# The last product of an attention and two-MLP kernel as seven block products over pairs of 384-token sets

## The chip, the cores and the metric

The kernel runs on one core of a Trainium2 chip. The metric is the time of one execution on the device, in microseconds (us). Before the change it is 973.07 us, the median of three runs (972.98 to 973.09).

## The reference

Causal block attention (4 batches, 8 heads, 576 positions, head size 64, blocks of 64) gives 2304 tokens of 512 values. Two small networks follow, both in float32:

```python
    a = x @ w1
    b = x @ w2
    h = a * b @ w3
    return (h @ w_out).astype(np.float32)
...
    h = x @ w_in
    alpha = 1.0
    g = np.where(h > 0.0, h, alpha * (np.exp(np.minimum(h, 0.0)) - 1.0))
    return (g @ w_out).astype(np.float32)
```

In the second network x is 2304 x 512, w_in 512 x 2048 and w_out 2048 x 512. The change touches only this second network, above all its last product `g @ w_out`.

## The kernel before, in words

Every float32 matrix product is made of three TensorE passes: each operand is split into a rounded high part (type fp32r) and the low remainder, and the passes are high x high, high x low and low x high (`PASSES`). The high part is written by ACT (a cast, L769), the remainder by POOL (a subtraction, L772).

The work has three stages that overlap at their borders. Stage 1 is the attention. Stage 2 (`block2`, eight sets of 288 tokens) is the first network; its matmuls are the groups a, b (L846) and y (L810), 288 columns wide. Stage 3 (`block3`, from L904) is the second network, in six sets of 384 tokens. In each set there are 16 hidden blocks of 128. For each block, 12 matmuls of 384 columns make `h` (L918: 4 blocks of the inner size times 3 passes, the weights are the stationary operand). DVE takes min(h, 0) (L930), ACT the exponential (L934), DVE joins both to g in place (L939), ACT and POOL split g. Then 9 matmuls of 512 columns (L953: 3 groups of 128 tokens times 3 passes) add this block to three output banks; g is the stationary operand there, and `w_out` the moving one. After block 15 the three banks are copied out (L439 on ACT, L440 on DVE) and written by DMA (L970). That is 1152 `h` matmuls and 864 `o` matmuls in stage 3.

The weights of stage 3 come as float64 words. During stage 2 a chain of small operations turns them into float32 and splits them (`convert`: loads L386, DVE L360 to L368, POOL L374, ACT L405, and the remainder L383 on POOL or DVE). Four of the sixteen weight slabs stay in SBUF (`slab_hi`); twelve go to DRAM (L1034) and come back (L1039) into the slabs of stage 2 as these fall free, once, before or early in stage 3. The inputs of stage 3 are split twice buffered: `xa` for even sets, `xb` for odd ones (L892, L897).

The order of the work is written by a planner (`Plan.run`): it goes through all operations with estimated durations, takes at each moment the ready operation with the lowest `prio` on each engine, and emits each engine's instructions in that order. The engines then run their queues strictly in it. Operations marked `port=True` are laid out so that DVE and POOL never do two of them at once. Some have `ways`, and the planner picks the engine. `TURNS` replaces the priority of single operations by hand-set numbers.

## Time and profile before

| | before |
|---|---|
| time, median of 3 runs | 973.07 us |
| span of the profiled execution (first to last instruction) | 970.1 us |
| PE busy | 960.6 us (99%) |
| DVE, ACT, POOL busy | 511.3, 427.6, 399.2 us |
| PE's granted clock | full speed in every slice of the page |
| stage 3 on PE, from its first stretch of `h` alone to the last `o` | 563.59 to 966.04 us |

The time around the span is 973.07 - 970.1 = 2.97 us. Stage 2 ends at about 563 us: from 557 us on, its last `y` matmuls and the first `h` matmuls alternate.

### The profile page before, as it was taken

What the parts mean: (1) busy time and instruction counts of PE and PEld (TensorE: products, weight loads), DVE (VectorE), ACT (ScalarE), POOL (GpSimd) and SP (SyncE); (2) the same over time, 40 slices, a digit from 0 to 9 for tenths busy, and PEclk for the clock granted to TensorE, in tenths of its full rate; (3) what the DMA queues carried; (4) which work ended last, traced back from release to release, by engine and by line L of the source; (5) the groups of instructions that cost most, each with busy time, mean ns of one, the idle gap of its engine ahead of it and who ended that gap; (6) DMA issues with size and microseconds to landing.
All of it is one profiled execution on the core that took longest, in us unless ns stands there. A gap on an engine that the chain in (4) does not pass through costs nothing.

```text
span 970.1 us, 15899 instructions
## 1 busy us (share of the span) xinstructions
PE 960.6 (99%) x5910; PEld 821.4 (85%) x5910; DVE 511.3 (53%) x1087; ACT 427.6 (44%) x1008; POOL 399.2 (41%) x419
## 2 busy tenths in 40 slices
PE   9999999999999999999999999999999999999998
PEld 4555478788888889999999999998999889888997
DVE  7888988766565556676766342322322322322322
ACT  5867577556656654464454422222222222222222
POOL 6354758323232226666656542332322422422222
PEclk9999999999999999999999999999999999999999
DMA  8554433131122003245465950000000000000000
GB/s 290 195 184 161 160 128 96 54 96 50 50 78 71 27 16 112 95 154 183 171 210 202 391 233 1 1 32 1 23 12 1 25 10 1 33 1 1 33 1 33
DMA packets 41789, 87.61 MB, mean 90 GB/s; under 512 B 6000, under 2 KB 15472, under 8 KB 40176
## 3 DMA queue, kind: packets, MB, share of 16 engines
q1 hardware_dynamic: 41712, 86.60, 25.8%
q8 instruction: 46, 0.75, 0.3%
q14 instruction: 31, 0.25, 0.1%
HBM read 69.21 MB, written 17.38 MB: 89 GB/s over the span
## 4 chain that ended last, share of the span: by engine, by line
PE 93%; DVE 4%; DMA 1%; issue 1%; SPq 1%; POOL 0%; ACT 0%; POOLq 0%; DVEq 0%; ACTq 0%
PE h L918 21%; PE o L953 21%; PE b L846 10%; PE a L846 10%; PE y L810 10%; PE o L675 5%; PE s L549 4%; PE t L585 4%; PE wps L745 4%; PE spare L1054 3%; PE s L611 1%; DVE ct L368 1%; DVE ct L360 1%; PE t L645 1%; DMA scr<-rs 0%
## 5 line engine op out<-in xcount | busy, mean ns | idle before, releaser
L772 POOL TENSOR_TENSOR g<-e,g 128x384 fp32r<-128x384 f32 x96 | 97.4, 1016 | 276.6 <-ACT g L769 262.8
L930 DVE TENSOR_SCALAR e<-h 128x384 f32<-128x384 f32 x96 | 53.4, 557 | 221.6 <-PE h L918 210.1
L953 PE MATMUL o<-slab_lo,g 128*128 128x512 f32 x648 | 162.9, 396 | 0.0
L934 ACT ACTIVATE e<-e 128x384 f32<-128x384 f32 x96 | 50.4, 525 | 232.2 <-DVE e L930 232.2
L953 PEld LDWEIGHTS o<-slab_lo,g 128*128 128x128 f32 x648 | 121.1, 188 | 23.5
L810 PE MATMUL y<-g,slab_lo 128*128 128x288 f32 x768 | 118.9, 300 | 0.5 <-DVE xy L830 0.3
L846 PE MATMUL a<-xs,slab_lo 128*128 128x288 f32 x768 | 117.9, 298 | 0.0
L846 PE MATMUL b<-xs,slab_lo 128*128 128x288 f32 x768 | 117.1, 297 | 0.4 <-DVE af L863 0.4
L810 PEld LDWEIGHTS y<-g,slab_lo 128*128 128x128 f32 x768 | 106.5, 188 | 2.7 <-issue 1.0
L846 PEld LDWEIGHTS b<-xs,slab_lo 128*128 128x128 f32 x768 | 106.7, 188 | 1.4 <-DVE af L863 0.6
L846 PEld LDWEIGHTS a<-xs,slab_lo 128*128 128x128 f32 x768 | 106.9, 188 | 1.0 <-issue 0.3
L772 POOL TENSOR_TENSOR g<-af,g 128x288 fp32r<-128x288 f32 x64 | 56.0, 875 | 80.0 <-ACT g L769 78.4
L918 PE MATMUL h<-xb,slab_lo 128*128 128x384 f32 x432 | 82.1, 339 | 0.0
L918 PE MATMUL h<-xa,slab_lo 128*128 128x384 f32 x432 | 81.5, 336 | 0.0
L939 DVE SCALAR_TENSOR_TENSOR e<-e,h 128x384 f32<-128x384 f32 x96 | 53.1, 554 | 51.2 <-ACT e L934 50.9
L918 PEld LDWEIGHTS h<-xb,slab_lo 128*128 128x128 f32 x432 | 77.1, 188 | 3.0
L918 PEld LDWEIGHTS h<-xa,slab_lo 128*128 128x128 f32 x432 | 76.3, 188 | 3.2 <-DVE e L939 0.2
L769 ACT CAST g<-e 128x384 fp32r<-128x384 f32 x96 | 49.0, 513 | 66.2 <-DVE e L939 58.2
L374 POOL TENSOR_TENSOR ct<-ct,cr 128x512 int32<-128x512 int32 x48 | 65.2, 1362 | 30.3 <-DVE ct L368 11.5
L575 ACT ACTIVATE p<-s,st 128x128 f32<-128x128 f32 (+3 forms) x128 | 67.2, 528 | 16.1 <-DVE st L570 11.4
L570 DVE TENSOR_REDUCE st<-s 128x1 f32<-128x128 f32 (+3 forms) x128 | 61.4, 489 | 5.5 <-PE s L555 2.1
L439 ACT COPY pt<-t 128x512 f32<-128x512 f32 (+4 forms) x91 | 36.8, 409 | 55.9 <-PE t L585 49.1
(89 smaller groups left out, 1455.7 us busy)
## 6 DMA issues: line engine op xcount, KB each, us to landing
cr<-w SPq DMA_DIRECT2D x48, 512.0 KB
wsc<-stage SPq DMA_DIRECT2D x24, 512.0 KB
slab_lo<-wsc SPq DMA_DIRECT2D x12, 1024.0 KB
cr<-w3T SPq DMA_DIRECT2D x16, 512.0 KB
raw<-qT SPq DMA_DIRECT2D x16, 288.0 KB
raw<-kT SPq DMA_DIRECT2D x16, 288.0 KB
out<-ob SPq DMA_DIRECT2D x17, 256.0 KB
cr<-wo SPq DMA_DIRECT2D x8, 512.0 KB
```

Of the source, the lines that this page charges most:

```text
L374: nc.gpsimd.tensor_tensor(out=t(), in0=t(), in1=words()[0], op=ALU.add)
L570: nc.vector.tensor_reduce(out=nm(c), in_=s()[:, 0:nk], axis=AX.X, op=ALU.max, negate=True)
L575: lambda s=s, c=c, p=p: nc.scalar.activation(out=p()[:, 0:nk], in_=s()[:, 0:nk], func=AF.Exp, bias=nm(c), scale=1.0, accum_out=sm(c)),
L769: add("ACT", act_us(n, True), lambda: nc.scalar.copy(g()[:, 0, :], src()), r=[key], w=[(g, 0)], prio=prio)
L772: lambda: nc.gpsimd.tensor_tensor(out=g()[:, 1, :], in0=src(), in1=g()[:, 0, :].bitcast(F32), op=ALU.subtract),
L810: nc.tensor.matmul(ps()[:, 0:T2], lhsT=w[:, a, n * P:(n + 1) * P], rhs=gs[m]()[:, c, :], start=(m == ms[0] and q == 0), stop=(m == ms[-1] ...
L846: nc.tensor.matmul(ps()[:, 0:T2], lhsT=w[:, a, u, k, :], rhs=xs()[:, k, c, :], start=(k == 0 and q == 0), stop=(k == KD - 1 and q == 2),)
L918: nc.tensor.matmul(ph()[:, 0:T3], lhsT=w[:, a, k, :], rhs=xs()[:, k, c, :], start=(k == 0 and q == 0), stop=(k == KD - 1 and q == 2),)
L930: "DVE", dve_us(T3), lambda e=e, ph=ph: nc.vector.tensor_scalar_min(e(), ph()[:, 0:T3], 0.0),
L934: "ACT", act_us(T3, True), lambda e=e: nc.scalar.activation(out=e(), in_=e(), func=AF.Exp),
L939: lambda e=e, ph=ph: nc.vector.scalar_tensor_tensor(out=e(), in0=e(), scalar=-1.0, in1=ph()[:, 0:T3], op0=ALU.add, op1=ALU.max),
L953: nc.tensor.matmul(acc(), lhsT=g()[:, a, s * P:(s + 1) * P], rhs=w[:, c, :], start=(m == 0 and q == 0), stop=(m == KG - 1 and q == 2),)
```

## The change

Two sets of 384 tokens are now worked as a pair, and `g` of a pair and `w_out` are cut into 2 x 2 blocks: the hidden size into halves of 1024, the output into halves of 256, the tokens into the two sets. The product of two such 2 x 2 block matrices needs eight block products; Strassen's identity (in Winograd's form) makes it with seven, p1 to p7, and sums of blocks before and after.

Stage 3 becomes six parts j: three pairs, and for each the hidden size in two steps of four blocks out of each half (`KP = 4`). `part_h(j)` makes 16 hidden blocks (4 q, 2 sets s, 2 halves f) exactly as before up to g, which is now kept unsplit in SBUF (`ga` for even j, `gb` for odd j). `part_o(j)` runs the seven terms of `TERMS`; for each of them and each q a block of g or a sum of blocks (`tt`, on DVE or POOL) is split into `sp` (ACT cast, remainder on POOL or DVE; six buffers), and 2 x 3 matmuls of 384 columns follow. Here the weights are stationary, g moves, and the output comes out transposed (the host turns it back). `post` adds the seven results up with DVE (and a few on POOL). `h` matmuls have four banks in place of two.

The seven weight combinations of `w_out` are made during stage 2 (`w_out_unit`: three subtractions, two ACT casts and four remainder subtractions for each of eight units) and written to DRAM (`wso`, eight units x 2 x 896 KB), as is `w_in` (`wsi`). In stage 3 both are read back piece by piece: 24 loads of `win` and 42 of `wout`, 1 MB each, into three buffers each. The split inputs have one buffer for each set of the pair. The hand-set priorities from operation 2498 on fall away, those before it stay.

```diff
+KP = 4
+NH = 256
+TERMS = ((0, "p1"), (6, "p6"), (2, "p2"), (5, "p7"), (4, "p5"), (1, "p4"), (3, "p3"))
...
-    2368: 17069.46, 2369: 17098.29, 2377: 17057.62, 2414: 17086.71, 2420: 17154.84, 2498: 1324.98, 2520: 2001.81,
...
-    3780: 106909.16, 3792: 106919.16,
+    2368: 17069.46, 2369: 17098.29, 2377: 17057.62, 2414: 17086.71, 2420: 17154.84,
...
-    hi_ring = Ring(late1, "slab_hi", 4, [P, 2, 1024], F32R, "gate1")
-    hi_buf = [hi_ring.next() for _ in range(4)]
...
-    wsc = [dram.tile([P, 2, 1024], F32, name=f"wsc{m}") for m in range(4, KG)]
+    wt_r = Ring(late1, "wt", 2, [P, 7, NH], F32, "gate1")
+    wh_r = Ring(late1, "wh", 2, [P, 7, NH], F32R, "gate1")
+    wsi = [dram.tile([P, 2, 2, HS], F32, name=f"wsi{m}") for m in range(KH)]
+    wso = [dram.tile([7, P, KP, 2, NH], F32, name=f"wso{p}") for p in range(NP)]
...
-    xs3_r = [Ring(late1, "xa", 1, [P, KD, 2, T3], F32R, "gate1"), Ring(late2, "xb", 1, [P, KD, 2, T3], F32R, "gate2")]
-    g3_r = Ring(late2, "g", 4, [P, 2, T3], F32R, "gate2")
...
+    win_r = slabs((8, 9, 10), "win", [P, 2, 2, HS], F32R)
+    wout_r = slabs((11, 6, 7), "wout", [P, KP, 2, NH], F32R)
+    xa_r = Ring(late1, "xa", 1, [P, KD, 2, T3], F32R, "gate1")
+    e_r = Ring(late1, "e", 3, [P, T3], F32, "gate1")
+    xb_r = slabs((4, 5), "xb", [P, 2, 2, T3], F32R)
...
+        ga = slabs((0, 1, 2, 3), "ga", [P, KP + 1, T3], F32)
+        late["ga"] = [ga.next() for _ in range(4)]
+        late["gb"] = Ring(late2, "gb", 1, [P, 4 * KP, T3], F32, "gate2").next()
+        late["sp"] = [after(r, "sp", [P, 2, T3], F32R) for r in (cr2_ring, stage_r, wh_r)]
+        late["ob"] = after(t2_ring, "ob", [P, T3], F32)
+        late["ot"] = [x.next() for x in [after(wt_r, "ot", [P, 4, T3], F32)] for _ in range(2)]
+        late["cp"] = xy_buf(0, "cp", (P, 6, T3))
...
+    def part_h(j, xs):
...
+            for s in range(2):
+                for f in range(2):
+                    ph = turn("h", (4, 5, 6, 7), "h")
...
+                            "PE", 6 * T3 * COL + 0.02, mm, r=[(wb, 0), *xkeys(k0), *xkeys(k0 + 1)], w=[ph],
+                            prio=1e5 + 1000 * j + 240 * q + 120 * s + 60 * f, lag=0.3, big=True,
...
+                        "DVE", dve_us(T3), lambda e=e, ph=ph: nc.vector.tensor_scalar_min(e(), ph()[:, 0:T3], 0.0),
...
+    def part_o(j):
...
+        zb = [bank((0, 2)[n], "oz") for n in range(2)]
+        xb = [bank((1, 3)[n], "ox") for n in range(2)]
...
+        for x, (slot, name) in enumerate(TERMS):
+            wb = wout_r.next()
+            add(
+                "SP", 0, lambda wb=wb, slot=slot: nc.sync.dma_start(out=wb().bitcast(F32), in_=wso[p][slot]),
...
+                if name == "p1":
+                    pr = need + 60
+                    tt(a21, a21, a11, ALU.subtract, [k11], [k21], pr, False)
+                    tt(a21, a21, a22, ALU.add, [k22], [k21], pr, False)
+                if name in ("p7", "p5", "p3"):
+                    s_, ks = sum_next()
+                    u, v, op, ku, kv = {
+                        "p7": (a22, a21, ALU.subtract, k22, k21),
+                        "p5": (a21, a11, ALU.add, k21, k11),
+                        "p3": (a12, a21, ALU.subtract, k12, k21),
+                    }[name]
+                    tt(s_, u, v, op, [ku, kv], [ks], need, False)
+                else:
+                    s_, ks = {"p1": (a11, k11), "p6": (a21, k21), "p2": (a12, k12), "p4": (a22, k22)}[name]
+                sp = split_next()
...
+                    "ACT", act_us(T3, True), lambda sp=sp, s_=s_: nc.scalar.copy(sp()[:, 0, :], s_()), r=[ks],
...
+                    "POOL", 0.17 + T3 * 0.00215,
+                    lambda lo=lo, hi=hi, s_=s_: nc.gpsimd.tensor_tensor(out=lo(), in0=s_(), in1=hi(), op=ALU.subtract),
+                    r=[ks, (sp, 0)], w=[(sp, 1)], prio=need, port=True,
+                    ways=[(
+                        "DVE", dve_us(T3),
...
+                for n in range(2):
+
+                    def mm(n=n, q=q, sp=sp, wb=wb, to=to, first=first, last=last):
+                        w = wb()[:, q]
                             nc.tensor.matmul(
+                                to[n]()[:, 0:T3], lhsT=w[:, a, n * P:(n + 1) * P], rhs=sp()[:, c, :],
...
+                        "PE", 3 * T3 * COL + 0.01, mm, r=[(wb, 0), (sp, 0), (sp, 1)], w=[to[n]],
+                        prio=1e5 + 1000 * (j + 1) + 34 * (KP * x + q) + 17 * n, lag=0.3, big=True,
+                    )
+            for n in range(2):
+                post(j, name, n, V(to[n]), to[n], fast)
-                    w = slab3(m)[:, :, 512:1024]
-                            acc(), lhsT=g()[:, a, s * P:(s + 1) * P], rhs=w[:, c, :],
...
+    def post(j, name, n, acc, ak, fast):
...
+            tt(ob, acc, a, ALU.add, [ak, ka], [ob], fast, True)
+            r0, t0 = (n + 2 * (i % 2)) * P, (A, Bt)[i // 2]
...
+        if name == "p1":
+            evac(T3, p1, acc, [ak], [k1], fast, "ACT")
+        elif name == "p6":
+            tt(u2, acc, p1, ALU.add, [ak, k1], [k2], fast, True)
+            more(u2, k2, 1)
+        elif name == "p2":
+            result(0, None, None)
+        elif name == "p7":
+            tt(u3, acc, p1, ALU.add, [ak, k1], [k3], fast, True)
+            more(u3, k3, 3)
+            more(p1, k1, 2)
+        elif name == "p5":
+            result(3, u3, k3)
+        elif name == "p4":
+            result(2, p1, k1)
+        else:
+            result(1, u2, k2)
...
-    first3 = [block3_in(t) for t in range(2)]
...
+    def w_in_unit(m, prio):
...
+    def w_out_unit(m, prio):
+        wt, wh = wt_r.next(), wh_r.next()
...
+        dtt(lambda t: t[:, 4:6], lambda t: t[:, 1:4:2], lambda t: t[:, 0:2], (0, 1, 3), (4, 5), 512)
+        dtt(lambda t: t[:, 6], lambda t: t[:, 3], lambda t: t[:, 4], (3, 4), (6,), 256)
+        dtt(lambda t: t[:, 1], lambda t: t[:, 2], lambda t: t[:, 6], (2, 6), (1,), 256)
+        for c0, c1 in ((4, 7), (0, 4)):
+            cs = range(c0, c1)
...
+                    "POOL", 0.17 + NH * (x1 - x0) * 0.00215, lambda sub=sub: sub(nc.gpsimd), r=[(wh, x) for x in xs_],
...
+                    out=wso[p_][:, :, q_, c, :].rearrange("i p c -> p i c"), in_=b().bitcast(F32)
...
+    for p in range(NP):
+        for q in range(KP):
+            for f in range(2):
+                w_in_unit(KP * p + q + f * KH, 2000.0 + 20 * p + q)
+        for q in range(KP):
+            w_out_unit(KP * p + q, 2010.0 + 20 * p + q)
+    stage3()
+    for j in range(NP * N3):
+        if j and j % NP == 0:
+            xs3 = [block3_in(j // NP * 2 + s) for s in range(2)]
+        part_h(j, xs3)
+        if j:
+            part_o(j - 1)
+    part_o(NP * N3 - 1)
```

Three places show how the instructions move. The first is PE in the middle of stage 3. Before, for one hidden block: `h` matmuls of one weight slab, then nine `o` matmuls with g as the stationary operand (the number behind `<-` first is the stationary slab or the moving tile, with its buffer number).

```order
L918 MATMUL h_7696<-xb_7037,slab_lo_1340 128x384 x6
L953 MATMUL o_7555<-slab_lo_1254,g_7684 128x512 x3
L953 MATMUL o_7560<-slab_lo_1254,g_7684 128x512 x3
L953 MATMUL o_7566<-slab_lo_1254,g_7684 128x512 x3
L918 MATMUL h_7696<-xb_7037,slab_lo_1340 128x384 x6
L918 MATMUL h_7725<-xb_7037,slab_lo_1417 128x384 x6
```

In the changed kernel, in part 1 of `part_h` and part 0 of `part_o` (`oz`, `ox`, `oy` are the output banks, two of each):

```order
L1069 MATMUL oz_7408<-sp_7500,wout_6860 128x384 x3
L984 MATMUL h_7614<-xb_6968,win_7304 128x384 x6
L984 MATMUL h_7614<-xb_6929,win_7304 128x384 x6
L1069 MATMUL oz_7402<-sp_7528,wout_6860 128x384 x3
L1069 MATMUL oz_7408<-sp_7528,wout_6860 128x384 x3
L1069 MATMUL ox_7486<-sp_7538,wout_7474 128x384 x3
L984 MATMUL h_7650<-xb_6968,win_7304 128x384 x6
L984 MATMUL h_7650<-xb_6929,win_7304 128x384 x6
L1069 MATMUL ox_7492<-sp_7538,wout_7474 128x384 x3
L1069 MATMUL ox_7486<-sp_7566,wout_7474 128x384 x3
```

Groups of three `o` matmuls now stand between groups of twelve `h` matmuls; all are 384 columns wide, and each six of `o` need one `sp`.

The second place is DVE in the middle of stage 3. Before, it only alternates the two operations of a hidden block:

```order
L930 TENSOR_SCALAR e_8558<-h_8507 128x384
L939 SCALAR_TENSOR_TENSOR e_8558<-e_8558,h_8507 128x384
L930 TENSOR_SCALAR e_8594<-h_8568 128x384
L939 SCALAR_TENSOR_TENSOR e_8594<-e_8594,h_8568 128x384
L930 TENSOR_SCALAR e_8623<-h_8587 128x384
```

In the changed kernel, in the last fifth of stage 3, from one `e<-h` on:

```order
L996 TENSOR_SCALAR e_10034<-h_10012 128x384
L1005 SCALAR_TENSOR_TENSOR gb_7434<-e_10034,h_10012 128x384
L1060 TENSOR_TENSOR sp_10057<-ga_7058,sp_10057 128x384
L959 TENSOR_TENSOR ga_7344<-ga_7344 128x384
L959 TENSOR_TENSOR ga_7058<-ga_7058 128x384
L996 TENSOR_SCALAR e_10074<-h_10049 128x384
L432 COPY cp_7641<-oz_9852 128x384
L1005 SCALAR_TENSOR_TENSOR gb_7434<-e_10074,h_10049 128x384
L959 TENSOR_TENSOR gb_7434<-gb_7434 128x384
L959 TENSOR_TENSOR ga_7166<-ga_7166 128x384
```

Remainders (L1060), sums of g blocks (L959) and the joining of results stand between the two operations of a hidden block, in one queue. The remainder into sp_10057 stands behind `h_10012`; PE uses that `sp` four hidden blocks later.

The third place is DVE where stage 2 ends. Before, the last of the weight conversion (`ct`, L368) is done ahead of the first `e`:

```order
L363 TENSOR_SCALAR ct_6823<-ct_6823 128x512
L863 TENSOR_TENSOR af_6833<-b_6825,af_6833 128x288
L368 SCALAR_TENSOR_TENSOR ct_6823<-cr_6746,ct_6823 128x512
L863 TENSOR_TENSOR af_6894<-b_6887,af_6894 128x288
L830 TENSOR_TENSOR xy_3750<-y_6904,xy_3750 128x288
```

In the changed kernel the last weight units (`ct`, `wt`) stand among the first hidden blocks:

```order
L1005 SCALAR_TENSOR_TENSOR ga_7058<-e_7032,h_6983 128x384
L1199 TENSOR_TENSOR wt_6916<-wt_6916 128x512
L1199 TENSOR_TENSOR wt_6916<-wt_6916 128x256
L822 TENSOR_TENSOR xy_3748<-y_7060,xy_3748 128x288
L996 TENSOR_SCALAR e_7088<-h_7048 128x384
L1199 TENSOR_TENSOR wt_6916<-wt_6916 128x256
L1005 SCALAR_TENSOR_TENSOR ga_7058<-e_7088,h_7048 128x384
L996 TENSOR_SCALAR e_7112<-h_7081 128x384
L360 SCALAR_TENSOR_TENSOR ct_7011<-cr_6931,ct_7011 128x512
L1215 TENSOR_TENSOR wt_6916<-wt_6916,wh_7079 128x512
```

The last operation on `wt` in this queue stands behind the thirteenth `e<-h` of stage 3, and the first `o` matmul stands behind 17 of the 96 groups of twelve `h` matmuls on PE.

## Rows read from the trace of the kernel before

**Rows 1.** The page: span, busy time of each engine, PE's clock by slice.
```profile
span 970.1 us, 15899 instructions
PE 960.6 (99%) x5910; PEld 821.4 (85%) x5910; DVE 511.3 (53%) x1087; ACT 427.6 (44%) x1008; POOL 399.2 (41%) x419
...
PEclk9999999999999999999999999999999999999999
```
**Rows 2.** PE's longest waits: releaser, us in total, times, longest us.
```profile
PE spare L1054 <- POOL mk L982: 2.0, 1, 2.0
PE t L585 <- ACT p L575: 1.8, 1, 1.8
PE o L675 <- DVE pt L440: 0.5, 1, 0.5
PE b L846 <- DVE af L863: 0.4, 1, 0.4
...
```
**Rows 3.** Busy us (instructions) by stretch: PE, PEld, DVE, ACT, POOL; clock, DMA share, GB/s.
```profile
300.00:400.00 100.00, 99.72 (x770) 88.79 (x769) 57.60 (x149) 52.10 (x140) 38.83 (x41) 1.00 0.19 62
400.00:500.00 100.00, 99.66 (x747) 99.39 (x746) 72.48 (x121) 49.88 (x103) 64.49 (x60) 1.00 0.49 169
500.00:560.00 60.00, 59.86 (x448) 59.62 (x447) 30.45 (x58) 25.98 (x54) 34.14 (x32) 1.00 0.75 282
562.00:570.00 8.00, 8.00 (x47) 7.45 (x47) 7.37 (x16) 2.13 (x5) 4.05 (x6) 1.00 1.01 422
600.00:700.00 100.00, 100.00 (x500) 90.15 (x499) 31.60 (x58) 26.49 (x51) 32.26 (x32) 1.00 0.03 11
```
**Rows 4.** PE in order of time: start, us, operation, count (an end is modelled).
```profile
535.04 1.76 PE L846 MATMUL a<-xs,slab_lo 128*128 128x288 f32 x12
536.64 1.76 PE L846 MATMUL b<-xs,slab_lo 128*128 128x288 f32 x12
...
563.59 4.33 PE L918 MATMUL h<-xa,slab_hi 128*128 128x384 f32 x24
567.76 2.27 PE L953 MATMUL o<-slab_hi,g 128*128 128x512 f32 x9
...
587.80 2.26 PE L953 MATMUL o<-slab_lo,g 128*128 128x512 f32 x9
589.90 2.26 PE L918 MATMUL h<-xa,slab_lo 128*128 128x384 f32 x12
```
**Rows 5.** The end, in order of time.
```profile
956.03 10.01 PE L953 MATMUL o<-slab_lo,g 128*128 128x512 f32 x42
...
966.13 0.42 DVE L440 COPY ob<-o 128x256 f32<-128x256 f32 x1 [2.17 <-PE o L953]
966.59 0.37 ACT L439 COPY ob<-o 128x256 f32<-128x256 f32 x1 [3.44 <-DVE ob L440]
```
**Rows 6.** Groups from 560 to 970 us: busy us, mean ns; idle before.
```profile
L772 POOL TENSOR_TENSOR g<-e,g 128x384 fp32r<-128x384 f32 x96 | 97.4, 1016 | 276.6 <-ACT g L769 262.8 <-issue 13.8
...
L930 DVE TENSOR_SCALAR e<-h 128x384 f32<-128x384 f32 x96 | 53.4, 557 | 221.6 <-PE h L918 210.1 <-POOL g L772 11.6
L939 DVE SCALAR_TENSOR_TENSOR e<-e,h 128x384 f32<-128x384 f32 x96 | 53.1, 554 | 51.2 <-ACT e L934 50.9
L934 ACT ACTIVATE e<-e 128x384 f32<-128x384 f32 x96 | 50.4, 525 | 232.2 <-DVE e L930 232.2
L769 ACT CAST g<-e 128x384 fp32r<-128x384 f32 x96 | 49.0, 513 | 66.2 <-DVE e L939 58.2 <-PE o L953 8.0
...
L918 PEld LDWEIGHTS h<-xb,slab_hi 128*128 128x128 f32 x144 | 25.7, 188 | 1.1
```
**Rows 7.** Groups from 400 to 575 us, the weight conversion's.
```profile
L374 POOL TENSOR_TENSOR ct<-ct,cr 128x512 int32<-128x512 int32 x26 | 35.2, 1357 | 19.1 <-issue 10.8 <-DVE ct L368 4.3 <-POOL g L772 2.0
...
L383 POOL TENSOR_TENSOR stage<-ct,stage 128x512 fp32r<-128x512 f32 x14 | 19.2, 1371 | 5.0 <-ACT stage L405 5.0
...
L383 DVE TENSOR_TENSOR stage<-ct,stage 128x512 fp32r<-128x512 f32 x10 | 8.9, 890 | 1.6 <-ACT stage L405 1.6
...
L383 DVE TENSOR_TENSOR slab_hi<-ct,slab_hi 128x512 fp32r<-128x512 f32 x2 | 2.0, 1010 | 0.0
```
**Rows 8.** Waits of the queue that issues the DMAs: us, times, longest.
```profile
SPq L386 <- POOL ct L374: 117.3, 36, 7.0
```

## What was predicted

> **What bounds the kernel now.** I read the page first: PE is busy 960.6 of 970.1 us, with its clock at full speed in all 40 slices, while DVE has 53%, ACT 44% and POOL 41% [rows 1]. Since a busy PE need not be PE at its pace, the waits come next: the longest single one is 2.0 us, and none of the listed ones stands in stage 3 [rows 2]. The stretches then show who else could bound a stage: in stage 3 (600 to 700 us) PE is busy for all 100 us, DVE for 31.60, ACT 26.49, POOL 32.26, and the DMAs move 11 GB/s; in stage 2 (400 to 500) DVE has 72.48 and POOL 64.49 [rows 3]. So stage 3 is bound by PE's stream alone, and a matmul column taken out there is time taken out, until another engine's queue is late.
>
> What a column costs follows from the starts of PE's stretches, since the ends are modelled. From 563.59 us [rows 4] to 956.03 + 10.01 = 966.04 [rows 5] PE issues 864 `o` matmuls of 512 columns and 1152 - 12 = 1140 `h` matmuls of 384 (twelve stand before 563.59): 864 x 512 + 1140 x 384 = 880,128 columns in 402.45 us, 0.4573 ns a column. So 384 columns take 175.6 ns, 512 take 234.1 ns. Three stretches confirm that the price goes by columns: 24 `h` take 567.76 - 563.59 = 4.17 us (173.8 ns each), nine `o` take 589.90 - 587.80 = 2.10 us (233 ns), and twelve matmuls of 288 columns in stage 2 take 536.64 - 535.04 = 1.60 us (133 ns) [rows 4].
>
> **The change part by part.** *PE in stage 3.* The 864 `o` matmuls of 512 columns go: 864 x 0.2341 = 202.3 us. In come 3 pairs x 2 steps x 7 terms x 4 blocks x 2 output halves x 3 passes = 1008 of 384 columns: 1008 x 0.1756 = 177.0 us. The 1152 `h` matmuls stay. Sum: -25.3 us. At the 173.8 ns of the pure stretch the whole stage (2160 matmuls) would take 375.4 us against 402.45 + 12 x 0.1756 = 404.6, that is -29.2 us; this is the far end of the gain.
>
> *DVE, POOL and ACT in stage 3.* DVE keeps 96 minima and 96 joinings: 96 x 0.557 + 96 x 0.554 = 106.7 us [rows 6]. The order gives it 85 remainders and 107 sums with two SBUF inputs, 66 additions from PSUM and 3 copies. For a 384-wide addition with a PSUM input the nearest row is the 0.554 us joining [rows 6]. An operation with two SBUF inputs of 384 does not occur: below, 0.554 us; above, the 512-wide remainder at 0.890, or 1.010 for two of them [rows 7]. I take 0.56, since width and type match that row, and keep 1.01 for the range. DVE: 106.7 + 192 x 0.56 + 69 x 0.554 = 252 us of the stage's 379 (67%); at 1.01 it is 339 us (89%). POOL has 83 remainders and 31 sums at 1.016 [rows 6]: 116 us (31%). ACT: 96 x 0.525 + 168 x 0.513 [rows 6] and 15 copies of about the same size: 144 us (38%). None reaches PE's 379 us. In the steady part the six `sp` let a remainder stand four hidden blocks ahead of its use (the order's second place), over 8 us, and four banks hold `h`: a late DVE operation of one microsecond does not reach PE. At the two changes of pair, `xa` is split only after its last use; between that and the first new `h` the order puts 54 matmuls (9.5 us) on PE, and the splits take four or eight POOL operations, some 4 to 5 us by the 1.016 of rows 6. I count 1 us for all of this, 0 to 8.
>
> *The end.* After the last `h` PE has 177 `o` matmuls (31.1 us) and nothing beside them, where before it had 42 (10.01 us [rows 5]). There DVE has about 28 two-input operations and 12 PSUM additions, POOL 12: laid end to end without overlap, 28 x 0.56 + 12 x 0.554 + 12 x 1.016 = 34.5 us; DVE alone 22. A cast, a remainder and a sum per `sp` must keep up with 1.05 us of PE. I count 1 us, 0 to 6. After PE's last matmul come two additions of 0.55 us in place of copies of 0.42 and 0.37 [rows 5], and the same kind of DMA: nothing.
>
> *Weight preparation in stage 2.* Added on DVE: 8 subtractions of 512 and 16 of 256, remainders 20 of 512 and 5 of 256; gone: 7 remainders. At 0.89 for 512 and half for 256: 28 x 0.89 + 21 x 0.45 - 7 x 0.89 = 28 us more, in a stretch (400 to 560) where DVE is busy 72.48 of 100 and 30.45 of 60 us [rows 3]: room for 57. POOL: 9 remainders at 1.371 go and 7 come, about even. The chain is paced by POOL already: the loads wait 117.3 us for it [rows 8]. So preparation runs on into stage 3 (the third place), covered by 17 groups of twelve `h` (17 x 12 x 0.1756 = 35.8 us) that need no `sp`. Behind a DVE operation on `wt` that waits for a DMA stand the minima of the next `h`, and behind these PE once four banks are full (4 x 2.1 us). I count 1 us, 0 to 15.
>
> *DMA.* 66 loads of 1 MB over 379 us are 183 GB/s by count, where the trace reached 422 GB/s at the border of the stages [rows 3]. Each has its buffer free while two others are in use (9 us or more): hidden. Without the cover a load costs about 1.05 MB / 422 GB/s = 2.5 us and its latency.
>
> *Sum*, against the profiled execution: 970.1 - 25.3 + 1 + 1 + 1 = 947.8 us of span, and with the 2.97 us around it, 950.8. **I predict 951 us**, 22 below the median of 973.07.
>
> **The rivals.** *The queue at the border (D).* DVE stands on a weight unit whose DMA is late, and PE runs dry in its first 40 us of stage 3. For it: DVE's and POOL's load in rows 3, the waits of rows 8, the full DMA at 562 us. Against: 35.8 us of cover and priority for the old stage's work. Price 8 to 15 us: 959 to 966 us.
>
> *The end or the collisions (C).* Two-input operations at 0.89 to 1.01: DVE reaches 316 to 339 us of 379 on the mean, and in the last 31 us 28 x 0.89 + 12 x 0.554 = 31.6, so that it paces PE there. For it: in the conversion the 512-wide remainder takes DVE 0.890 and 1.010 us [rows 7], more than its width explains (0.554 x 512 / 384 = 0.74). Against: the planner keeps these operations of DVE and POOL apart. Price 5 to 10 us: 956 to 961. The Trainium skill's page "SBUF — State Buffer", section "SBUF: two separate sides", says that a DVE operation with two SBUF inputs and a GpSimd operation exclude each other for their whole length; the rows of 0.890 and 1.010 agree with it. By that rule the last 31 us hold one queue of 28 x 0.56 + 12 x 1.016 = 27.9 us beside PE's 31.1, and C would come out as the forecast does.
>
> *The weight loads bind (W).* 2160 loads of the stationary operand stand in for 2016. In 600 to 700 us PEld is busy 90.15 us for 499 loads, 180.7 ns each [rows 3]; priced so, stage 3 takes 390.3 us, a gain of only 14.3: 961.8 us with the 3 us. Against: 24 matmuls with 24 loads in 4.17 us, and 769 loads in 88.79 us [rows 3, 4], 115 ns each. The Trainium skill, page "Trainium Kernel Development and Optimization", section "Best Practices", calls the busy share of the weight loads, not that of the matmuls, the measure of how near PE is to its limit. By that rule the stage is 90% full and the price is W's; the trace does not agree, since 288-column matmuls pass at 133 ns.
>
> *DVE becomes the bound (S), slower than before.* In-order DVE takes the stage over if a two-input operation costs more than (404.6 - 106.7 - 38.2) / 192 = 1.35 us on the mean. At 1.5 us the stage lasts 433 us and the kernel 1001. For it: operations lengthen where POOL is busy (1.010). Against: nothing in the rows reaches 1.35.
>
> *The change does not do what it says* is out for PE: the order has the 1008 matmuls of 384.
>
> **How the numbers follow.** Forecast 0.70 (946 to 956 us; with every stall at zero 947.8, or 943.9 at 173.8 ns). C 0.12, D 0.10, W 0.03, S 0.05. The range 945 to 962 us holds the forecast, C, W and the cheap part of D; outside are the pure gain, the dear part of D and S, in all under 0.2. A measurement of this kernel can tell about 0.2% (2 us) from no change. Slower is S, 0.05; 0.02 of D is left for stalls that eat just what is gained, the same; faster is the rest, 0.93.
>
> **What would show it.** Right: 1008 matmuls at 175 ns, PE full from the first `h` to the end, stage 3 some 380 us long; DVE about two thirds busy, two-input operations near 0.56; PE's waits in stage 3 3 us in all. Wrong: PE waiting for DVE or POOL on `sp` in many places (C, S), a gap within 40 us of the first `h` (D), or PE full with `o` at 181 ns (W). A stage 2 longer than before would be outside all of these.

## The result, and the profile after

The changed kernel takes 944.27 us (median of four runs, 942.28 to 946.19); the kernel before, on the same chip, 973.03. The ratio is 0.9717, 95% interval 0.9694 to 0.974. The forecast was 951 us, 945 to 962: the direction and the mechanism came true, and the gain was 29 us where 22 were expected, so that the time lies 0.7 us below the range.

First the page of the changed kernel, the same lines as [rows 1]:

```profile
span 943.7 us, 16752 instructions
PE 930.5 (99%) x6054; PEld 830.7 (88%) x6054; DVE 684.3 (73%) x1378; ACT 463.3 (49%) x1088; POOL 423.8 (45%) x435
...
PEclk9999999999999999999999999999999999999999
```

The span fell by 26.4 us (970.1 to 943.7), PE's busy time by 30.1, though PE has 144 instructions more. DVE went from 511.3 to 684.3 us and is still not what the end waits for. The profiled run took 945.47 us, 1.77 more than its span. Of the four runs, the two with a mean granted clock of 1.000 took 942.28 and 943.07 us, the two with 0.998 took 945.47 and 946.19. The profiled one shows where its clock was lower: right behind a wait of 2.26 us in the attention, at 0.50, which is the lower of the two levels (1.2 in place of 2.4 GHz; columns as in [rows 4] and [rows 3]):

```profile
73.94 1.54 PE L577 MATMUL t<-ident,p 128*128 128x128 f32 x6 [2.26 <-ACT p L567]
...
74.00:76.00 2.00, 2.00 (x9) 1.52 (x10) 1.56 (x3) 2.00 (x6) 0.92 (x1) 0.50 0.61 234
```

The kernel before has such a stretch as well (0.50 from 76 to 78 us, behind a wait of 1.79 us). The page does not show it, since its digit 9 stands for 0.9 or more: "full speed in every slice" was more than it says.

PE's waits in the changed kernel, columns as in [rows 2]:

```profile
PE oz L1069 <- ACT e L1000: 2.6, 2, 2.4
...
PE spare L1254 <- POOL mk L1136: 2.0, 1, 2.0
PE y L802 <- DVE xy L822: 1.7, 2, 1.5
```

The first row is new and stands in stage 3, the last one at the end of stage 2. Nothing else there is longer than half a microsecond. The stretches (columns as in [rows 3]):

```profile
400.00:500.00 100.00, 99.81 (x749) 99.57 (x747) 73.27 (x133) 49.26 (x97) 55.17 (x54) 1.00 0.58 193
500.00:560.00 60.00, 58.49 (x437) 58.26 (x436) 42.13 (x76) 26.99 (x56) 32.82 (x34) 1.00 0.78 283
560.00:600.00 40.00, 40.00 (x238) 40.00 (x237) 31.05 (x58) 16.72 (x30) 23.99 (x23) 1.00 0.65 209
600.00:700.00 100.00, 100.00 (x578) 100.00 (x578) 77.56 (x133) 36.27 (x77) 40.61 (x39) 1.00 0.52 185
700.00:800.00 100.00, 97.60 (x564) 97.31 (x563) 71.11 (x128) 35.05 (x73) 34.39 (x36) 1.00 0.54 191
```

PE is full from 560 to 700 us and loses 2.40 us in 700 to 800. In 600 to 700 it starts 578 matmuls of 384 columns, one every 100 / 578 = 0.173 us. The order of time on PE says the same and shows the loss:

```profile
566.55 4.32 PE L984 MATMUL h<-xb,win 128*128 128x384 f32 x24
570.71 4.32 PE L984 MATMUL h<-xa,win 128*128 128x384 f32 x24
...
781.31 1.73 PE L1069 MATMUL oy<-sp,wout 128*128 128x384 f32 x9
785.43 0.76 PE L1069 MATMUL oz<-sp,wout 128*128 128x384 f32 x3 [2.40 <-ACT e L1000]
...
914.92 4.32 PE L1069 MATMUL ox<-sp,wout 128*128 128x384 f32 x24
919.08 4.32 PE L1069 MATMUL oz<-sp,wout 128*128 128x384 f32 x24
923.24 4.32 PE L1069 MATMUL ox<-sp,wout 128*128 128x384 f32 x24
```

24 matmuls from 566.55 to 570.71 are 4.16 us, 173.3 ns each; at the end, from 914.92 to 919.08, it is the same, with no `h` beside it. So in stage 3 every matmul now goes at about the pace of the fastest stretch that [rows 4] had (173.8), not at the mean of the mixed stream (175.6) on which the sum was built. The account of the span, with each matmul taken from its start to the next start: stage 3 took 404.2 us before and takes 377.5 now (2159 x 0.1733 = 374.2, and 3.3 us of waits), -26.7; stage 2 +0.9; from the start of PE's last matmul to the end of the span 3.8 us in place of 4.4, -0.6. Together -26.4.

What held PE at 783 us is read on DVE in the same microseconds:

```profile
781.49 1.02 DVE L944 CAST xb<-xy 128x384 fp32r<-128x384 f32 x2
782.44 1.36 DVE L959 TENSOR_TENSOR gb<-gb 128x384 f32<-128x384 f32 x1
783.72 0.55 DVE L996 TENSOR_SCALAR e<-h 128x384 f32<-128x384 f32 x1
784.19 0.68 DVE L944 CAST xb<-xy 128x384 fp32r<-128x384 f32 x1
784.79 0.55 DVE L959 TENSOR_TENSOR cp<-oy,ot 128x384 f32<-128x384 f32 x1
```

`oz` of the new step uses the banks that `oy` of the old one has just filled. The addition that empties the first of them ends at 785.34 and PE starts at 785.43. It stood behind casts of the new pair's inputs (`xb`) and behind a sum of g blocks that took 1.36 us in place of 0.55, beside POOL:

```profile
782.33 2.32 POOL L949 TENSOR_TENSOR xb<-xy,xb 128x384 fp32r<-128x384 f32 x2 [0.29 <-DVE xb L944]
```

The releaser that the wait's row names (ACT's `e`) is then not the one that counts; the run with exchanged banks, below, tests that.

DVE's groups from 560 to 944 us, as in [rows 6] (busy us, mean ns):

```profile
L1060 DVE TENSOR_TENSOR sp<-ga,sp 128x384 fp32r<-128x384 f32 x55 | 36.3, 663 | 24.3 <-ACT sp L1049 23.7
L959 DVE TENSOR_TENSOR ga<-ga 128x384 f32<-128x384 f32 x48 | 30.8, 662 | 1.1 <-POOL ga L960 0.7
...
L959 DVE TENSOR_TENSOR gb<-gb 128x384 f32<-128x384 f32 x24 | 24.0, 1000 | 0.4
...
L959 DVE TENSOR_TENSOR ot<-ox,ot 128x384 f32<-128x384 f32 x27 | 14.7, 556 | 2.8 <-PE ox L1069 2.8
```

With a PSUM operand 0.556, as expected; with two SBUF operands 0.55 to 1.10 by group, over all 192 some 135 us, 0.70 each where 0.56 was put in.

### The profile page after: what moved, and what is told of

It reads as the page before. It is cut to its first block, busy times and chain, and to the rows that moved or that the text cites. A ratio compares the mean times of both kernels' runs of the same rounds, so it can differ in the third digit from the quotient of the medians.

```text
span 943.7 us, 16752 instructions
## 1 busy us (share of the span) xinstructions
PE 930.5 (99%) x6054; PEld 830.7 (88%) x6054; DVE 684.3 (73%) x1378; ACT 463.3 (49%) x1088; POOL 423.8 (45%) x435
## 2 busy tenths in 40 slices
DMA packets 60659, 154.79 MB, mean 164 GB/s; under 512 B 7072, under 2 KB 33696, under 8 KB 52128
## 4 chain that ended last, share of the span: by engine, by line
PE 91%; DVE 4%; DMA 2%; issue 1%; ACT 0%; POOL 0%; SPq 0%; POOLq 0%; ACTq 0%; DVEq 0%
PE h L984 21%; PE y L802 10%; PE b L838 10%; PE a L838 10%; PE ox L1069 8%; PE wps L737 5%; PE o L667 5%; PE oz L1069 5%; PE oy L1069 5%; PE s L541 4%; PE t L577 4%; PE s L603 2%; DMA cr<-w 1%; PE t L637 1%; DMA cr<-w3T 1%
## 5 line engine op out<-in xcount | busy, mean ns | idle before, releaser
L1056 POOL TENSOR_TENSOR sp<-ga,sp 128x384 fp32r<-128x384 f32 x65 | 65.9, 1016 | 151.7 <-ACT sp L1049 144.2
L1049 ACT CAST sp<-ga 128x384 fp32r<-128x384 f32 x120 | 61.1, 511 | 103.0 <-PE ox L1069 55.5
L984 PE MATMUL h<-xa,win 128*128 128x384 f32 x576 | 107.6, 334 | 0.0
L984 PE MATMUL h<-xb,win 128*128 128x384 f32 x576 | 107.1, 334 | 0.0
L984 PEld LDWEIGHTS h<-xb,win 128*128 128x128 f32 x576 | 100.5, 188 | 0.0
L984 PEld LDWEIGHTS h<-xa,win 128*128 128x128 f32 x576 | 100.4, 188 | 0.0
L1069 PE MATMUL ox<-sp,wout 128*128 128x384 f32 x432 | 83.1, 334 | 0.0
L1069 PEld LDWEIGHTS ox<-sp,wout 128*128 128x128 f32 x432 | 75.6, 188 | 0.0
L346 ACT ACTIVATE ct<-cr 128x512 f32<-128x512 f32 x67 | 45.4, 678 | 41.6 <-DMA cr<-w 22.8
L737 PE MATMUL wps<-full,full 128*128 128x512 f32 x128 | 58.5, 596 | 0.0
```

What stands on the lines that cost most here:

```text
L737: nc.tensor.matmul(ps(), lhsT=a[:, j, :], rhs=bb, start=(j == 0), stop=(j == KF - 1))
L984: nc.tensor.matmul(ph()[:, 0:T3], lhsT=w[:, a, k, :], rhs=x(k, c), start=(k == 0 and i == 0), stop=(k == KD - 1 and i == 2),)
L1049: "ACT", act_us(T3, True), lambda sp=sp, s_=s_: nc.scalar.copy(sp()[:, 0, :], s_()), r=[ks],
L1056: lambda lo=lo, hi=hi, s_=s_: nc.gpsimd.tensor_tensor(out=lo(), in0=s_(), in1=hi(), op=ALU.subtract),
L1069: nc.tensor.matmul(to[n]()[:, 0:T3], lhsT=w[:, a, n * P:(n + 1) * P], rhs=sp()[:, c, :], start=(first and q == 0 and i == 0), stop=(q == K ...
```

## The experiments

The pitch of a matmul is the mean distance from one start to the next in the trace, gaps over 300 ns left out. In stage 3 (last 330 us) it is 175.7 ns (`h`) and 234.0 (`o`, 512 columns) in the kernel before. All ratios are to the kernel before on the same chip (971.72, 971.06, 970.44 and 970.53 us in the four groups of runs). The changed kernel itself was measured only beside its own 973.03, so that a variant is compared with it by ratio, or by what the traces show.

**First group: where do the 5 us above the sum come from?** The kernel before without the hand-set priorities of stage 3:

```diff
-    2368: 17069.46, ... 2420: 17154.84, 2498: 1324.98, ... 3792: 106919.16,
+    2368: 17069.46, ... 2420: 17154.84,
```

> The kernel before, with the hand-set priorities from operation 2498 on taken out, as the change does; the matmuls stay the same. If these priorities are worth little: 973 to 974 us. Rival: the changed kernel lost a hand-set order worth 3 us or more, then this is 976 us or more. It is also the base for the next run.

Measured 973.34 us, ratio 1.0026 (1.0012 to 1.004), pitch 176.3 and 234.0. That part of the change costs 2.5 us by itself (by the ratio), and the slow pitch does not come from the hand-set order. Then also the product turned round, still with eight blocks:

```diff
-    acc(), lhsT=g()[:, a, s * P:(s + 1) * P], rhs=w[:, c, :],
+    acc()[:, 0:T3], lhsT=w[:, a, s * P:(s + 1) * P], rhs=g()[:, c, :],
```

> As the run before, with all eight block products, but the last product turned round: w_out is the stationary operand, g moves 384 wide (1152 matmuls of 384 in place of 864 of 512, the same columns), the output transposed. Theory: before pays 175.6 and 234.1 ns for 384 and 512 columns where the changed kernel pays 173.3 ns, and this comes from g being the stationary operand: stage 3 becomes 2304 x 0.1733 = 399.3 in place of 404.6 us, 5 us less than the run before, about 968 us. Rival: the pitch comes from something else (two banks for h, the conversion, the memory of the operands): the same time as the run before within 1.5 us.

Measured 976.09 us, ratio 1.0048 (1.0032 to 1.0064). The theory that stationary weights are faster falls: `h` keeps 176.5, and `o`, now 384 wide, takes 176.6. PE in order of time, of this kernel:

```profile
700.31 3.31 PE L912 MATMUL h<-xa,slab_hi 128*128 128x384 f32 x18
703.46 2.28 PE L947 MATMUL o<-g,slab_hi 128*128 128x384 f32 x12
705.58 2.27 PE L912 MATMUL h<-xa,slab_hi 128*128 128x384 f32 x12
```

Twelve `o` from 703.46 to 705.58 are 176.7 ns each, eighteen `h` before them 175.0, with PE never waiting; the changed kernel does the same shapes in 173.3. This kernel has 2304 matmuls of 384 in stage 3, the changed one 2160: 144 x 0.1733 = 25.0 us is the identity's own part, and 2304 x 3.2 ns = 7.4 us goes with the pitch.

Two variants of the changed kernel look at its waits. The first gives `oy` banks of its own and leaves `h` two:

```diff
-    ph = turn("h", (4, 5, 6, 7), "h")
+    ph = turn("h", (6, 7), "h")
-    yb = [bank((0, 2)[n], "oy") for n in range(2)]
+    yb = [bank((4, 5)[n], "oy") for n in range(2)]
```

> The changed kernel with banks 4 and 5 for p5 and p3 (oy) and two banks in place of four for h. Theory: the one stall of 2.4 us in stage 3 is p1 of the next part waiting for the bank pair 0 and 2 that DVE has still to empty of p3; with a pair of its own it goes, and the time is 941 to 943 us. Rival: two banks for h make PE wait for DVE at every h: 947 us or more, with many short waits of h on e.

Measured 949.08 us, ratio 0.9775 (0.9756 to 0.9794). The wait of `oz` is gone from its list of waits, and others came for it:

```profile
PE y L802 <- DVE xy L822: 2.5, 2, 2.3
...
PE h L984 <- DVE ga L1005: 1.7, 3, 1.1
PE oy L1069 <- DVE sp L1060: 1.0, 1, 1.0
```

The theory's 941 to 943 us is missed and the rival's figure met: four banks for `h` are worth more than separate banks for `oy`. The second puts every remainder and sum of stage 3 on DVE:

```diff
-    more = [] if psum_in or not ways else [("POOL", 0.17 + T3 * 0.00215, pool, True)]
+    more = []
...
-    "POOL", 0.17 + T3 * 0.00215,
+    "DVE", dve_us(T3),
```

> The changed kernel with all remainders and sums of stage 3 on DVE, none on POOL: 168 + 204 in place of 85 + 173. Theory: two-input operations of DVE took 0.70 us on the mean in place of 0.55 because POOL held the shared SBUF port; without POOL they take 0.55 to 0.58 and DVE is busy some 325 of 377 us (86%); PE still sets the time, 943 to 950 us. Rival: they are slow for another reason (the 1.00 us of sums inside one tile stay): DVE passes 377 us and the kernel takes 960 us or more.

Measured 946.01 us, ratio 0.9749 (0.973 to 0.9768): 114 operations more on DVE and hardly a difference. Its groups and a stretch:

```profile
L1056 DVE TENSOR_TENSOR sp<-ga,sp 128x384 fp32r<-128x384 f32 x120 | 65.3, 555 | 13.2 <-ACT sp L1049 12.2
L959 DVE TENSOR_TENSOR gb<-gb 128x384 f32<-128x384 f32 x24 | 14.1, 586 | 0.1
```

```profile
600.00:700.00 100.00, 99.26 (x571) 98.69 (x571) 83.42 (x162) 35.61 (x76) 8.94 (x8) 1.00 0.56 203
```

With POOL at 8.94 of 100 us the same operations take 0.555 and 0.586 us where they took 0.663 and 1.000 beside a POOL at 40.61. At one and the same width, the length of a two-input operation goes by what POOL does meanwhile.

**Second group: the place of the operands, and room on DVE.** The slow pitch seemed to go with tiles high up in SBUF. One pool, which PE does not read in these stages, goes to the top and pushes the others down; the instructions keep their order:

```diff
-    xyp = ctx.enter_context(tc.tile_pool(name="xyp", bufs=1))
+    xyp = ctx.enter_context(tc.tile_pool(name="xyp", bufs=1, side="right"))
```

> The changed kernel with one pool, the four residual tiles xy that TensorE never reads, moved from byte 99968 of each partition to the top (192480 and up). Every instruction stays where it was in the order; the tiles allotted after xy move down by 32 to 37 KB, so that xs and g of stage 2 lie at 167136 to 192480 in place of 204000 to 229344. In the changed kernel as it was, matmuls whose streaming operand is xs or g take 133 to 134 ns for 288 columns, 3 to 3.5 above 288 times the 0.4514 ns a column of stage 3; all other tiles lie below 196 KB and show no excess. Theory (the place of the operand decides): the some 1900 matmuls of stage 2 lose 3.3 ns each, 6 us: 938 (936 to 940). Rival (the excess belongs to the instruction sequence or to 288 columns): no change, 944 (942 to 946).

> The kernel before with the same one edit, the instruction order unchanged. Its xb and g of stage 3 lie at 204768 to 229344, and go down to 167904 to 192480. Theory (the place decides): stage 3 goes from 404.6 to 399.3 us (173.3 and 231.1 ns a matmul) and stage 2 gains the 6 us as well: 962 (960 to 964); the real gain of the product in seven blocks is then the pure column count, some 24 us, in either placement. Rival (the sequence): 972 to 973, h still at 176 and o at 234 ns.

Measured 947.48 us (ratio 0.9762, 0.9739 to 0.9786; span 943.7, as without the edit) and 970.87 (0.9994, 0.9982 to 1.0005), with pitches of 133.3 in stage 2 and 175.7 and 234.0 in stage 3. The height does nothing; the theory falls. (The first median is 3.2 us above that of the changed kernel, at the same span of the profiled run: its four runs had a granted clock of 0.996 to 0.998, those of the changed kernel 0.998 to 1.000.)

The changed kernel without the 75 block sums of g (a plain block stands in for the sum):

```diff
-    tt(a21, a21, a11, ALU.subtract, [k11], [k21], pr, False)
-    tt(a21, a21, a22, ALU.add, [k22], [k21], pr, False)
...
-    tt(s_, u, v, op, [ku, kv], [ks], need, False)
```

> The changed kernel without the block sums of g in stage 3 (75 additions and subtractions with two SBUF inputs): the products p1, p3, p5, p6 and p7 take a plain block instead of a sum, so their values are not the reference's; all matmuls, remainders and output additions stay. Theory (the sums lie beside TensorE and cost only the stall of 2.4 us at the change of pair): 941 to 944. Rival (C of the prediction: the collisions with GpSimd hold TensorE back): under 940.

Measured 942.62 us, ratio 0.9705 (0.9689 to 0.9722), span 941.0: all those sums cost TensorE under 3 us, and the wait of 2.40 us is gone. And the opposite, each SBUF sum once more on DVE:

```diff
+    nc.vector.tensor_tensor(out=k(), in0=a(), in1=b(), op=op)
```

> The changed kernel with each of the sums that read two SBUF tiles (block sums, output sums) done once more on VectorE, into a BF16 tile that nobody reads: 138 operations more. VectorE stood at 73% of 100 us in stage 3, some 276 of 377; with 138 times 0.56 to 0.75 it comes to 353 to 380 us. Theory (a stage is TensorE's until VectorE's own sum passes it, and local queues show first): 948 to 957, with TensorE waits on sp and g. Rival (room enough): 944 to 946. Rival S (in-order VectorE makes TensorE late for each operation added): over 960.

Measured 960.08 us, ratio 0.989 (0.987 to 0.9911), above every figure of the first theory and at the edge of rival S. DVE is busy 85 to 88% of the stretches of 100 us, so it is not full; the time goes at the end, where no `h` stands between the terms:

```profile
930.39 1.62 PE L1076 MATMUL ox<-sp,wout 128*128 128x384 f32 x6 [0.17 <-issue]
936.94 0.69 PE L1076 MATMUL oy<-sp,wout 128*128 128x384 f32 x1 [4.93 <-ACT sp L1056]
...
951.20 2.27 PE L1076 MATMUL oy<-sp,wout 128*128 128x384 f32 x6 [2.30 <-DVE sp L1067]
```

Over 0.1733 us each, the distances between starts sum to 20.0 us in stage 3, against 3.3 in the changed kernel. Some 3.8 of it is PE's own clock: behind the waits of 2.06 (at 784 us), 4.93 and 2.30 us, 26 distances are 320 ns, and from 935 to 940 us the granted clock is 0.50. A local queue binds before the mean does.

**Third group.** The slow places all read a weight whose high and low parts lie 4096 bytes apart; the fast ones 2048 or 1024. Both kernels with 2048 in place of 4096 (the core of the edit):

```diff
-    "slab_lo", [P, 2, 1024], F32R
+    "slab_lo", [P, 2, 2, HS], F32R
```

> The changed kernel with the twelve slabs of stage 2 laid out so that the high and the low part of a weight block lie 2048 bytes apart in a partition in place of 4096; order of the work unchanged. In stage 3 of the changed kernel win has 2048 and wout 1024, and the matmuls take the pure 173.3 ns; every place that shows an excess of 2 to 4 ns (stage 2 of both kernels, stage 3 of the kernel before) reads an operand whose two parts lie 4096 apart. Theory (that distance makes the excess): the matmuls of stage 2 fall from 133.3 to 130.0 ns, and with some 1900 of them the time falls by up to 6 us, to 938 to 941. Rival (the excess goes by the sequence of instructions): pitch and time unchanged, 942 to 947.

> The kernel before with the same layout of its slabs, in stage 2 and in stage 3 alike (high and low 2048 bytes apart). Theory (the distance): h 173.3 and o 231.1 ns, stage 3 down by 5 us and stage 2 by up to 6, 961 to 964. Rival (the sequence of instructions): h 175.7, o 234.0 and the time of the kernel before, 970 to 973; then the 5 us belong to the order of the work, and no layout gives them.

Measured 948.74 us (0.9765, 0.9744 to 0.9787) and 971.52 (1.0008, 0.9998 to 1.0017), pitches 133.3, 175.7 and 234.0 as ever: this falls too. (In the first, two more gaps of over a microsecond stand at 932 and 941 us, and in 700 to 800 us the mean clock is 0.98: here the clock fell behind the wait of 2.40 us, which it did not in the changed kernel.)

The wait at 783 us, with the banks exchanged from step to step:

```diff
-    zb = [bank((0, 2)[n], "oz") for n in range(2)]
-    xb = [bank((1, 3)[n], "ox") for n in range(2)]
+    zb = [bank((j % 2, 2 + j % 2)[n], "oz") for n in range(2)]
+    xb = [bank((1 - j % 2, 3 - j % 2)[n], "ox") for n in range(2)]
```

> The changed kernel with the two pairs of PSUM banks of the output products exchanged from one step to the next (three constants). A step's first product then goes to the pair whose last addition ran one term (4.2 us) earlier, in place of the pair that the step before has just filled last. Theory (the stall of 2.40 us at the second change of pair is the wait for VectorE to empty that bank, which the trace's row puts down to ScalarE's e): the stall is gone, stage 3 2.4 us shorter, 941 to 943. Rival (it is the wait for e, or for sp): a stall of the same size stays, 943 to 946.

Measured 944.94 us (943.07 to 945.41), ratio 0.973 (0.9713 to 0.9748), span 941.3. At the same place of this kernel, and on DVE beside it:

```profile
781.97 1.72 PE L1069 MATMUL oy<-sp,wout 128*128 128x384 f32 x9
783.53 1.20 PE L1069 MATMUL oz<-sp,wout 128*128 128x384 f32 x6
```

```profile
783.10 1.37 DVE L959 TENSOR_TENSOR gb<-gb 128x384 f32<-128x384 f32 x1
...
785.48 0.54 DVE L959 TENSOR_TENSOR cp<-oy,ot 128x384 f32<-128x384 f32 x1
```

DVE's queue is as late as it was, and PE runs on: the wait was for the bank, as the theory said. Stage 3 took 374.5 us in place of 377.5 and the span shrank by 2.4; the time, with its spread of 2 us, does not show that and misses the theory's 941 to 943.

**Last run.** In the turned product, the slow operands (g, xb) begin at a byte of 32 modulo 64, and in stage 3 of the changed kernel all begin at a multiple of 64; the shift of 36864 bytes had kept that. A pad of 96 bytes mends it for stage 2, on top of the exchanged banks:

```diff
+    ctx.enter_context(tc.tile_pool(name="padp", bufs=1, side="right")).tile([P, 24], F32, name="pad")
```

> The kernel with alternating banks, and a pad of 96 bytes at the top of each partition, so that every tile of the upper pool (xs and g of stage 2) begins at a multiple of 128 bytes; it began at one of 32 modulo 64. The order of the work is that of the run with alternating banks. Seen so far: matmuls of 384 columns take 173.3 ns where all operands begin at a multiple of 64 (stage 3 of the changed kernel) and 176.7 where the streaming operand does not (g and xb in the transposed product), and the shift by 36864 bytes, itself a multiple of 64, changed nothing. Theory (the start of the operand modulo 64 makes the 3.3 ns): the matmuls of 288 columns in stage 2 fall from 133.3 to 130.0 ns, 2148 of them are 7 us, and the time falls to 935 to 938. Rival (the pitch is 13.3 ns and the columns at 2.4 GHz, and 133.3 is already pure): 133.3 stays, 941 to 945.

Measured 940.85 us (938.49 to 942.68), ratio 0.9694 (0.968 to 0.9709): below the run with banks alone, whose interval it does not touch, and the fastest of all. PE in stage 2, of this kernel and then of the changed kernel without the pad:

```profile
470.97 2.55 PE L839 MATMUL b<-xs,slab_lo 128*128 128x288 f32 x18
473.36 4.95 PE L803 MATMUL y<-g,slab_lo 128*128 128x288 f32 x36
478.14 0.96 PE L839 MATMUL a<-xs,slab_lo 128*128 128x288 f32 x6
```

```profile
473.32 2.56 PE L838 MATMUL b<-xs,slab_lo 128*128 128x288 f32 x18
475.72 4.56 PE L802 MATMUL y<-g,slab_lo 128*128 128x288 f32 x33
```

Eighteen take 473.36 - 470.97 = 2.39 us with the pad and 2.40 without, 36 take 4.78 (132.8 each); over 400 to 500 us the mean is 132.4 ns against 133.3. So the start of an operand does count, but for 0.9 ns and not for the 3.3 expected: neither theory has the size. Nor is the fall of the time the pad's alone. PE's order is the same in both kernels, so that the 4.6 us of span (941.3 to 936.7) can be placed. The first matmuls of stage 2, with banks alone and then with the pad:

```profile
129.11 1.87 PE L838 MATMUL a<-xs,slab_lo 128*128 128x288 f32 x12
```

```profile
126.17 1.85 PE L839 MATMUL a<-xs,slab_lo 128*128 128x288 f32 x12
```

2.9 us are won ahead of any matmul that reads a shifted tile: `t` in the attention waited 0.9 us in place of 2.1, and the granted clock from 60 to 80 us was 1.00 in place of 0.91. Of the other 1.7 us, 0.5 are a shorter wait of `y` (1.2 to 0.7), and some 1.2 are left for the pitch.

## Why the prediction came out as it did

*What bounds the kernel.* Right: PE's stream alone, before and after. The loads of 1 MB (all transfers together are 154.79 MB) hold nothing: no wait of PE names them.

*PE in stage 3: the term that was mis-sized.* It stood at -25.3 us, from a price of 0.4573 ns a column over the whole stage. 1008 matmuls of 384 came as counted, but at 173.3 ns, and the 1152 `h` matmuls, entered as unchanged, fell from 175.7 to 173.3 as well. So the stream lost 30.0 us (404.2 to 374.2) where 25.3 were forecast; with 1.3 us more of waits than counted and 0.6 less behind the last matmul, this is the miss of the span (943.7 against 947.8). The two numbers stood side by side in the working, 175.6 for the mixed stream and 173.8 for pure `h`, and the lower was taken for a far end; the stretches that were to confirm one price differ, 173.8 / 384 = 0.453 ns a column and 233 / 512 = 0.455. The choice that failed was to carry the mean of the old stream, which held something of its own, into a new one.

What the old stream paid for was looked for in five places. The hand-set order, the turn of the product, the height in SBUF and the distance of the two parts are out; the start of the operand modulo 64 moves stage 2 a little and was not tried in the kernel before. Its trace narrows the question: the tile that is read counts, and not only the mixture of `h` and `o`. The 24 `h` in a row of [rows 4] read `xa` and took 173.8 ns each; as many in a row that read `xb` took (761.45 - 757.21) / 24 = 176.7:

```profile
757.21 4.40 PE L918 MATMUL h<-xb,slab_hi 128*128 128x384 f32 x24
761.45 0.85 PE L953 MATMUL o<-slab_lo,g 128*128 128x512 f32 x3
```

Over the last 330 us it is 174.7 from `xa` and 176.4 from `xb`, where the changed kernel takes 173.3 from both. There `xb` and the `g` that PE reads have moved out of the upper pool, in which they began at 32 modulo 64. Whether that start is what makes 175.7 of 173.3 stays open.

*The time around the span.* The time missed by more than the span did, 6.5 us (944.27 against 950.8). The 2.97 us put the median of some runs against the span of another execution; in every run on record the time is 1.7 to 1.9 us above its own span. That is 1.2 us, and the profiled run stands 1.2 us above the median of its four. That the far end of the working (943.9 us, no stall at all) lies so near 944.27 is in part luck: it leaves out 3.3 us of waits, and its 2.97 us are too many.

*Waits in stage 3 and at the end.* Expected 1 + 1 us, measured 3.3, of which 2.40 are one wait at a change of pair. The place was named, the cause was not: PE did not wait for the split inputs, but for a bank shared by two steps, whose addition stood behind the splits in DVE's queue. At the end, 177 matmuls run with no wait over 0.2 us.

*Weight preparation.* Expected 1 us, 0 to 15; PE is full from 560 to 600 us, so rival D is out, and 1.5 us of waiting for `xy` on a fuller DVE (42.13 of 60 us against 30.45) stand at 554 us. That they come from the preparation was not tried alone.

*Two-input operations on DVE.* 0.56 was put in and 0.70 came, inside the bounds. Rival C had the mechanism and not the price: the collisions are there, and taking all block sums out gains under 3 us. The working had held against C that the planner keeps DVE and POOL apart; the queues run by their own times, and a `gb` sum of 1.36 us lies wholly beside two POOL operations. The Trainium skill, page "SBUF — State Buffer", section "SBUF: two separate sides", says that such a pair excludes each other for the whole instruction. The trace agrees: 0.663 and 1.000 us beside a busy POOL, 0.555 and 0.586 beside an idle one.

*Rival W.* Out: PEld is busy 100.00 us of 100 with 578 loads just where the pitch is at its lowest. The Trainium skill, page "Trainium Kernel Development and Optimization", section "Best Practices", names that share, beside MFU (the used share of the peak arithmetic), as the measure of the distance from PE's limit. Here it rose from 90.15 to 100.00 us while each matmul became shorter. A load is recorded with 188 ns in both kernels ([rows 6] and below), longer than the 173.3 from one matmul to the next, so that in the changed kernel the loads alone fill the time:

```profile
L984 PEld LDWEIGHTS h<-xb,win 128*128 128x128 f32 x576 | 100.5, 188 | 0.0
```

*Rival S.* The point was 1.35 us on the mean. No operation's mean reached it. The run with doubled sums shows that the point was set too high: 138 operations more cost 16 us (some 3.8 of them by PE's lower clock behind the waits) with DVE at 85 to 88%, since the queue at the end binds before the mean of the stage.

## What to carry to other kernels

Price the matmuls of a new stream by stretches of one kind, apart for each tile that they read (173.8 from `xa`, 176.7 from `xb`), and ask what the mean of the old stream contains, before that mean goes into a sum; give the range both ends. When a PSUM bank is filled last by one step and first by the next, whatever stands ahead of its reader in an in-order queue becomes a wait of PE; alternate the banks. Whether extra work on a second engine is covered is decided where its cover ends, not by its mean share. Where two kernels run PE in the same order, compare them matmul by matmul before a difference of a few microseconds is put down to the edit.

## What the runs showed of the hardware

The pitch of a matmul of the same shape, with PE never waiting, was 173.3 ns in one stream and 176.7 in another, stable from run to run and blind to a shift by 36864 bytes; in one kernel it was 173.8 from one tile and 176.7 from another. A shift by 96 bytes of the tiles that stage 2 reads took its matmuls from 133.3 to 132.4 ns. Behind a wait of PE of about 2 us its granted clock was 0.50 for some microseconds in several traces (matmuls of 384 columns 320 ns apart), and stayed at 1.00 behind the wait of 2.40 us in the changed kernel. A wait's row can name the wrong releaser: at 785.43 us it was the addition that empties the bank, not the exponential it gives.
